# Swapping the partition halves that the second head group's projection reads, in a fused Nyström attention and two-layer FFN kernel

## The chip, the cores and the metric

One core of a Trainium2 chip (trn2). The metric is the device time of one execution in microseconds (us). The engines are called as in the profile: PE is TensorE's matmuls, PEld its weight loads, DVE is VectorE, ACT is ScalarE, POOL is GpSimd, SP is SyncE, which here issues nearly all DMAs.

## The reference

q, k and v have the shape (4 batches, 8 heads, 576 rows, 64). Everything is float32.

```
q_lm, k_lm = means of q, k over runs of 18 rows        (32 landmarks)
A, Bm, C = softmax(q k_lm'), softmax(q_lm k_lm'), softmax(q_lm k')
Z = six Newton steps towards the inverse of Bm
x = A @ Z @ C @ v            -> 2304 tokens x 512
h = x @ moe_w_in  (512 x 2048);  g = h * tanh(softplus(h));  x = g @ moe_w_out
h = x @ moe2_w_in (512 x 2048);  g = h * sigmoid(h);         out = g @ moe2_w_out
```

## The kernel before, in words

The eight pairs of batch and head group (`Group`, line 1042; four heads in each, group 0 and group 1 of a batch) are worked through one after the other. For each, the kernel makes the 32 landmarks, the three softmaxes, the Newton steps, and at the end of `main` (lines 1284 to 1300) a small matrix per head, transposed: `ut_t[b][:, hg]` = (Z C v)' blocks of 64 rows by 32 columns. A head's block lies in one half of the 128 partitions: even heads in partitions 0 to 63, odd heads in 64 to 127. It is written by two matmuls into `pu`, one for the even heads and one for the odd, and one copy.

The attention output itself is never formed. Instead `projection` (lines 641 to 668) multiplies each head's 32 rows of Z C v with that head's 64 rows of `moe_w_in` (`w_t["a", ...]`, tile `wa`), for a block `fb` of 512 columns. The result, 4 heads x 32 = 128 partitions for each of the two groups `e`, goes to two PSUM banks `pp[0]` and `pp[1]` (tile `t` in the profile), is split there into a high and a low part (`wp`, by ACT or DVE), and is then the stationary operand against the softmax A (`at`) in `emit_h`. There are 4 batches x 4 blocks = 16 projections, each of 8 matmuls of 64 rows by 32 columns by 512: TensorE runs them on quarters of its columns and halves of its rows. Which row half a matmul uses follows from the partitions of its operands (`r`), and which column quarter from the partitions of its output (`32 * h`). In the order of the program, written as (row half, column quarter), a projection before runs (0,0) (1,1) (1,1) (0,2) (0,2) (1,3) (1,3) (0,0). Each float32 matmul is two instructions in the trace.

After attention starts, the first FFN layer (`emit_h`, `gated`, `emit_o`) fills TensorE between attention steps; partial sums go to DRAM (`yh`, `ys`). The second layer (`second_layer`, lines 896 to 915) runs one level of Strassen in a fixed order of matmuls.

The order of all other work is written out at build time by a planner (`Line`): it holds modelled times for each engine and for the DMA stream (`transfer`, line 259), and issues what is due. Engines then run their instructions in that order, and wait for data. `cost` (lines 103 to 108) gives a 64 x 32 matmul an eighth of the whole-array time. While attention runs and the model sees TensorE without work for a time, lines 1518 to 1526 insert pairs of transposes of `ident` into an unused bank (the instructions `y<-ident`, `h<-ident` and some `t<-ident` in the trace; nothing reads their output).

`loading` (lines 567 to 595) brings each weight from DRAM as 512 KB tiles of 128 partitions with one DMA each, from the SP queue. For `moe_w_in` there are 16 such tiles (`"a"`; `f = fb * 4 + kk`); kk = 0 and 1 hold group 0's heads, kk = 2 and 3 group 1's. The first two go to `wst`, the next four to `aw` (space that the softmax tiles use later), the rest to `wst`. `decode` (line 530) turns the loaded words into float32 in `wa` with ACT and DVE instructions.

The scores of the softmaxes A and C (`scores`, line 1122) also use 64 x 32 matmuls, 8 for each call, in the order (0,0) (1,1) (0,2) (1,3) (1,0) (0,1) (1,2) (0,3). The lines in the profile are those of the planner's helper: L256 is every computing instruction and L268 every DMA, so rows are told apart by tiles.

Of the kernel before, what the change touches and what calls it, by code (L numbers as in the profile page):

```python
# [55 lines left out]
def f32(ap):  # L56
    return ap.bitcast(FP32)


def width(ap):  # L60
    return ap.size() // ap.shape[0]


class Line:
# [194 lines left out]
    def transfer(self, engine, **kw):  # L259
        ap = kw["out"] if kw["out"].space == bass.MemoryType.SB else kw["in_"]  # L260
        start = max(self.now, self.free["D"], self.depend("D", "dma", kw))
        rate = 0.24e6 if ap.shape[0] < 128 else 0.4e6
        self.free["D"] = start + width(ap) * ap.shape[0] * 4 / rate
        end = self.free["D"] + 2.1
        self.end = max(self.end, end)
        self.last.add("D")
        self.record("D", kw, end)
        return engine.dma_start(**kw)  # L268
# [120 lines left out]
def kernel(  # L389
# [11 lines left out]
    nc = tc.nc  # L401
# [3 lines left out]
    LM = 32  # L405
# [3 lines left out]
    HG = 4  # L409
    GB = H // HG  # L410
# [3 lines left out]
    KD = DM // 128  # L414
# [12 lines left out]
    line = Ring.line = Line(nc)  # L427
# [11 lines left out]
    def slots(n, of, **kw):  # L439
# [30 lines left out]
        out=twice.rearrange("p (a d) -> p a d", a=2),  # L470
# [18 lines left out]
    def until(cond):  # L489
        while not cond():  # L490
            yield "W"

    def marked(*m):
        return lambda: all(a in marks for a in m)
# [4 lines left out]
    w_t, w_ready = {}, {}  # L499
# [10 lines left out]
    def place(o, l, f):  # L510

        if o == "a":
            fb = f // KD
            return wa_p, [] if fb < 2 else [("P", B - 1, fb - 2)]
        n = f if l == 0 else 2 * (f % HF) + f // HF
        if o == "i":
            i = 0 if n < HF else 1 + (n - HF) // (HF // 2)
            return wi_pools[i] if i < len(wi_pools) else None, []
        p = n // HF
        pool = w_pools[p][n % HF] if p in w_pools else None  # L520
        return pool, [] if l == 0 else [("last", n)]
# [45 lines left out]
    def loading():  # L567
        yield from until(marked(("load",)))
        for i, (o, l, f) in enumerate(w_order):
            yield from until(lambda: sum((w not in w_ready) for w in w_order[:i]) < LOADS)  # L570
            wst = None
            if o == "a":
                if f < 2 or not lent:
                    yield from until(wst_r.any)
                    wst = wst_r.take([128, 512, 2], I32)
                    a = wst[0]
                else:
                    a = lent.pop(0)
                fb, kk = divmod(f, KD)
                src = weights[l][0][kk * 128:(kk + 1) * 128, fb * 2 * FB:(fb + 1) * 2 * FB]  # L580
            elif o == "i":
                yield from until(lambda: place(o, l, f)[0] is not None and wst_r.any())
                wst = wst_r.take([128, 512, 2], I32)
                a = wst[0]
                src = weights[l][0][:, f * 256:(f + 1) * 256].rearrange("(k p) n -> p k n", p=128)
            else:
                yield from until(lambda: place(o, l, f)[0] is not None and marked(*place(o, l, f)[1])())
                a = place(o, l, f)[0].tile([128, 512, 2], I32, tag="w", name="wst")
                src = weights[l][1][f * 128:(f + 1) * 128, :]
            if o == "i":  # L590
                line.transfer(nc.sync, out=a.rearrange("p (k n) t -> p k (n t)", k=KD), in_=src)
            else:
                line.transfer(nc.sync, out=a.rearrange("p n t -> p (n t)"), in_=src)
            decodes.append((i, line.add(decode(o, l, f, a, wst), "D", "A", line.end)))
            yield "W"
# [16 lines left out]
    a_t, a_ready, ut_t, wp_t, wp_ready = {}, {}, {}, {}, {}  # L612
# [20 lines left out]
    def projections():  # L633

        for half in range(2):
            for b in range(B):
                yield from until(marked(*((b, "ut", e) for e in range(GB))))
                for fb in (2 * half, 2 * half + 1):
                    yield from projection(b, fb)

    def projection(b, fb):
        keys = [("a", 0, fb * KD + kk) for kk in range(KD)]
        yield from until(lambda: wp_r.any() and all(w_ready.get(k, LATE) <= line.now for k in keys))
        yield from until(lambda: t_r.claim(GB))
        pp = [t_r.take([128, FB], FP32) for e in range(GB)]
        for i in range(HG):
            for e in range(GB):
                h = (i + e) % HG
                r = slice(64 * (h % 2), 64 * (h % 2) + 64)
                T.matmul(  # L650
                    out=pp[e][0][32 * h:32 * h + 32],
                    lhsT=ut_t[b][r, e, h // 2, :],
                    rhs=f32(w_t[keys[2 * e + h // 2]])[r, :],
                    start=True,
                    stop=True,
                )
        marks.add(("P", b, fb))
        wp_ = wp_t[b, fb] = wp_r.take([128, 2, GB, FB], F32R)
        wp = wp_[0]
        yield "W"  # L660
        for e in range(GB):
            VA.copy(out=wp[:, 0, e], in_=pp[e][0])
        yield "V"
        for e in range(GB):
            V.tensor_tensor(out=wp[:, 1, e], in0=pp[e][0], in1=f32(wp[:, 0, e]), op=ALU.subtract)
            Ring.give(pp[e])
        wp_ready[b, fb] = line.end + 0.12 + SLACK
        yield "W"
# [373 lines left out]
    class Group:  # L1042
# [215 lines left out]
        def newton(self):  # L1258

            yu, g = self.yu, self.g  # L1260
            bd = self.bd.rearrange("p h l -> p (h l)")
            whole = g > 1
            for it in range(6):
                lo = 0 if it < 5 else LM
                if whole:
                    yield "V"
                    self.blocks(yu[:, 0:LM], 1.0)
                    yield "T"
                yield from until(self.banks.open)
                pn = self.banks.take([128, LM + D], FP32)  # L1270
                if whole:
                    T.matmul(out=pn[0][:, lo:], lhsT=bd, rhs=yu[:, lo:], start=True, stop=True)
                else:
                    self.each(pn[0][:, lo:], yu[:, 0:LM], yu[:, lo:])
                yield "V"
                yn = s_p.tile([128, LM + D], FP32, tag="yu", name="yu", bufs=4)
                V.scalar_tensor_tensor(
                    out=yn[:, lo:], in0=yu[:, lo:], scalar=2.0, in1=pn[0][:, lo:], op0=ALU.mult, op1=ALU.subtract
                )
                Ring.give(pn)  # L1280
                yu = yn
                yield "T"
            yield "V"
            self.blocks(self.bn, self.rc)
            yield "T"
            yield from until(self.banks.open)
            pu = self.banks.take([128, HG // 2 * LM], FP32)
            for e in range(2):
                T.matmul(
                    out=pu[0][64 * e:64 * e + 64].rearrange("p (i l) -> p i l", l=LM),  # L1290
                    lhsT=yu[:, LM:],
                    rhs=self.bd[:, e::2],
                    start=True,
                    stop=True,
                )
            yield "W"
            VA.copy(out=ut_t[self.b][:, self.hg].rearrange("p i l -> p (i l)"), in_=pu[0])
            Ring.give(pu)
            yield "W"
            marks.add((self.b, "ut", self.hg))  # L1300
            yield from until(marked((g, "a_t")))
            marks.add((g, "done"))
# [150 lines left out]

    line.add(attention(), "C")
    line.add(loading(), "S")
    line.add(projections(), "X")
    line.add(inputs(), "S")
# [8 lines left out]
    def o_time(u):  # L1466
        ph, t, f, first, last = u
        if first and not y_r.any_of(KD):
            return LATE
        return max(g_ready.get((ph, t, f), LATE), w_ready.get(("o", 0, f), LATE))  # L1470
# [4 lines left out]
    while todo or flight:  # L1475
# [15 lines left out]
        if f_r is not None and len(later) and wp_r.any():  # L1491
# [3 lines left out]
            n = 4 * TH if name else 2 * TH  # L1495
# [12 lines left out]
        to = o_time(flight[0]) if flight else LATE  # L1508
# [23 lines left out]
        ph, t, f, first, last = u  # L1532
# [56 lines left out]
```

## Time and profile before

| | |
|---|---|
| median of 3 runs | 850.13 us (850.02 to 850.81) |
| the profiled execution | 849.0 us |
| its span, first to last instruction | 847.2 us |
[...]
| PE busy | 828.9 us (98%), 5922 instructions |
| DVE, ACT, POOL busy | 532.3, 445.1, 281.8 us |
| DMA | 72.31 MB, mean 85 GB/s |

The page of the profile gives each engine's busy time, the span in slices, and the chain of waits: from the last instruction back to what released it, or to the instruction before it on its engine. In a chain or a timeline, "PE t L256 x16" is 16 instructions in a row that write tile `t`. A window's line gives each engine's busy time in a stretch. Matmul ends are modelled, so durations of overlapping small matmuls say less than the starts of what follows them.

### The profile page before, as it was taken

How to read it: one execution, taken by the hardware profiler on the slowest of the kernel's cores; microseconds unless marked ns; L12 is line 12 of the kernel's file. 1: busy time of each engine (PE TensorE's matmuls, PEld its weight loads, DVE VectorE, ACT ScalarE, POOL GpSimd, SP SyncE). 2: the span in 40 equal slices, each digit the busy share in tenths (PEclk: the TensorE clock that was granted, in tenths of full speed). 3: DMA queues.
4: the chain of work that ended last, by engine and by line, in shares of the span. 5: the costliest groups of instructions: out<-in, count | busy, mean ns of one | idle time of the engine just before them, and what ended most of it. 6: DMA issues, size and time to landing. Idle time of an engine off the chain costs nothing.

```text
span 847.2 us, 15580 instructions
## 1 busy us (share of the span) xinstructions
PE 828.9 (98%) x5922; PEld 735.2 (87%) x5922; DVE 532.3 (63%) x1088; ACT 445.1 (53%) x979; POOL 281.8 (33%) x324
## 2 busy tenths in 40 slices
PE   8999999999999999999999999999999999999997
PEld 6687978878899898989899898988888988998885
DVE  7968665664477787434407999877555567555542
ACT  6576765747465655433435665554444444544422
POOL 3323533442345565415333244221223221232210
PEclk9999999999999999999999999999999999999999
DMA  9664114200145465331117223101300000200002
GB/s 297 233 208 132 59 55 141 79 8 30 47 160 185 146 212 176 111 113 52 52 57 226 97 83 107 38 1 50 102 0 1 1 1 11 65 1 1 1 2 74
DMA packets 41483, 72.31 MB, mean 85 GB/s; under 512 B 4288, under 2 KB 30912, under 8 KB 41408
## 3 DMA queue, kind: packets, MB, share of 16 engines
q1 hardware_dynamic: 40832, 70.53, 26.1%
q8 instruction: 46, 0.75, 0.4%
q10 hardware_dynamic: 576, 0.79, 0.3%
q14 instruction: 29, 0.24, 0.1%
HBM read 57.15 MB, written 14.16 MB: 84 GB/s over the span
## 4 chain that ended last, share of the span: by engine, by line
PE 91%; DVE 3%; DMA 2%; ACT 2%; issue 1%; SPq 1%; DVEq 0%; ACTq 0%
PE y L256 49%; PE h L256 32%; PE t L256 10%; DMA wp<-in_q_dram 1%; SPq L268 1%; DVE z L256 0%; ACT z L256 0%; DMA wst<-ys 0%; DMA out_dram<-ysb 0%; DVE wa L256 0%; DVE at L256 0%; DVE nm L256 0%; ACT wp L256 0%; DVE asm L256 0%; ACT ysb L256 0%
## 5 line engine op out<-in xcount | busy, mean ns | idle before, releaser
L256 PE MATMUL y<-g,wo 128*128 128x288 f32 x1536 | 229.6, 300 | 0.0
L256 PEld LDWEIGHTS y<-g,wo 128*128 128x128 f32 x1536 | 209.0, 189 | 12.4 <-issue 11.3
L256 PE MATMUL y<-wo,xg 128*128 128x512 f32 x693 | 179.8, 395 | 0.0
L256 POOL TENSOR_TENSOR g<-z,g 128x288 fp32r<-128x288 f32 x127 | 112.7, 901 | 155.6 <-ACT g L256 114.5
L256 PEld LDWEIGHTS y<-wo,xg 128*128 128x128 f32 x693 | 128.6, 188 | 20.8
L256 DVE TENSOR_TENSOR z<-h,z 128x384 f32<-128x384 f32 x162 | 88.5, 554 | 67.6 <-PE h L256 65.0
L256 PE MATMUL h<-at,wp 128*128 128x288 f32 x768 | 120.8, 302 | 3.9 <-ACT z L256 3.7
L256 PEld LDWEIGHTS h<-at,wp 128*128 128x128 f32 x768 | 106.3, 188 | 12.1 <-ACT z L256 6.2
L256 ACT ACTIVATE z<-h 128x288 f32<-128x288 f32 x128 | 51.8, 413 | 70.4 <-PE h L256 65.6
L256 ACT ACTIVATE z<-z 128x384 f32<-128x384 f32 x94 | 49.4, 525 | 39.8 <-DVE z L256 39.4
L256 POOL TENSOR_TENSOR wo<-m,wo 128x512 fp32r<-128x512 f32 x32 | 47.3, 1480 | 47.6 <-ACT wo L256 39.6
L256 PE MATMUL h<-xg,wp 128*128 128x384 f32 x288 | 58.0, 336 | 1.5 <-DVE z L256 1.5
L256 PE MATMUL h<-xg,wf 128*128 128x384 f32 x288 | 57.7, 336 | 0.2 <-DVE z L256 0.2
L256 DVE TENSOR_TENSOR xg<-z,xg 128x384 fp32r<-128x384 f32 x75 | 43.2, 576 | 21.0 <-ACT xg L256 20.9
L256 DVE SCALAR_TENSOR_TENSOR m<-wst,m 128x512 int32<-128x512 int32 x64 | 55.4, 873 | 0.7
L256 PEld LDWEIGHTS h<-xg,wp 128*128 128x128 f32 x288 | 51.2, 188 | 5.1 <-DVE z L256 1.9
L256 PEld LDWEIGHTS h<-xg,wf 128*128 128x128 f32 x288 | 51.3, 188 | 3.6 <-DVE z L256 0.5
L256 ACT CAST g<-z 128x288 fp32r<-128x288 f32 x116 | 48.6, 435 | 8.7 <-PE y L256 7.5
L256 POOL TENSOR_TENSOR wf<-m,wf 128x256 fp32r<-128x256 f32 x20 | 15.2, 762 | 91.3 <-ACT wf L256 86.6
L256 PE MATMUL y<-wo,wp 128*128 128x512 f32 x171 | 44.9, 395 | 0.0
L256 DVE TENSOR_TENSOR wp<-t,wp 128x512 fp32r<-128x512 f32 x32 | 20.6, 685 | 33.6 <-ACT wp L256 33.6
L256 ACT ACT_TABLE_LOAD x31 | 39.8, 1283 | 3.3 <-PE h L256 2.0
(234 smaller groups left out, 1228.5 us busy)
## 6 DMA issues: line engine op xcount, KB each, us to landing
wst<-in_moe_w_out_dram SPq DMA_DIRECT2D x32, 512.0 KB, 6.0
wst<-in_moe_w_in_dram SPq DMA_DIRECT2D x28, 512.0 KB, 4.5
kn<-in_k_dram SPq DMA_DIRECT2D x8, 576.0 KB, 7.1
vn<-in_v_dram SPq DMA_DIRECT2D x8, 576.0 KB, 6.4
yh<-ysb SPq DMA_DIRECT2D x32, 144.0 KB, 1.8
ysb<-yh SPq DMA_DIRECT2D x32, 144.0 KB, 2.9
ys<-ysb SPq DMA_DIRECT2D x32, 144.0 KB, 2.2
qn<-in_q_dram SPq DMA_DIRECT2D x7, 576.0 KB, 4.8
```

Of the source, the lines that this page charges most:

```text
L256: r = getattr(self.nc[e], name)(**kw)
L268: return engine.dma_start(**kw)
```

## The change

The second group's weight rows (kk >= 2) are loaded with their two partition halves swapped, by two DMAs of 64 partitions instead of one of 128; the second group's `ut` blocks are written to the opposite halves by its two `pu` matmuls; and the projection takes, for group e and head i, the half (i + e) % 2. The projection's matmuls are then (0,0) (1,0) (1,1) (0,1) (0,2) (1,2) (1,3) (0,3). The planner's DMA model gives its lower rate only to transfers of exactly 96 partitions, no longer to all below 128; the other such transfers are the new halves (64) and the stores of the result (`send`, 32).

```diff
     def transfer(self, engine, **kw):
...
-        rate = 0.24e6 if ap.shape[0] < 128 else 0.4e6
+        rate = 0.24e6 if ap.shape[0] == 96 else 0.4e6
...
             if o == "i":
                 line.transfer(nc.sync, out=a.rearrange("p (k n) t -> p k (n t)", k=KD), in_=src)
+            elif o == "a" and kk >= KD // GB:
+                for e in range(2):
+                    to = a[64 * e:64 * e + 64].rearrange("p n t -> p (n t)")
+                    line.transfer(nc.sync, out=to, in_=src[64 - 64 * e:128 - 64 * e])
             else:
...
         for i in range(HG):
             for e in range(GB):
-                h = (i + e) % HG
-                r = slice(64 * (h % 2), 64 * (h % 2) + 64)
+                r = slice(64 * ((i + e) % 2), 64 * ((i + e) % 2) + 64)
                 T.matmul(
-                    out=pp[e][0][32 * h:32 * h + 32],
-                    lhsT=ut_t[b][r, e, h // 2, :],
-                    rhs=f32(w_t[keys[2 * e + h // 2]])[r, :],
+                    out=pp[e][0][32 * i:32 * i + 32],
+                    lhsT=ut_t[b][r, e, i // 2, :],
+                    rhs=f32(w_t[keys[2 * e + i // 2]])[r, :],
...
             for e in range(2):
+                r = slice(64 * ((e + self.hg) % 2), 64 * ((e + self.hg) % 2) + 64)
                 T.matmul(
-                    out=pu[0][64 * e:64 * e + 64].rearrange("p (i l) -> p i l", l=LM),
+                    out=pu[0][r].rearrange("p (i l) -> p i l", l=LM),
```

## Rows read from the trace of the kernel before

**Rows 1.** The page: busy us of each engine, share of the span, instructions.

```profile
PE 828.9 (98%) x5922; PEld 735.2 (87%) x5922; DVE 532.3 (63%) x1088; ACT 445.1 (53%) x979; POOL 281.8 (33%) x324
```

**Rows 2.** Windows: stretch, length, busy PE, PEld, DVE, ACT, POOL, clock, DMA share, GB/s.

```profile
40.00:130.00 90.00, 88.73 (x908) 75.20 (x898) 62.86 (x164) 63.47 (x125) 36.13 (x39) 1.00 0.36 113
130.00:230.00 100.00, 97.91 (x960) 82.90 (x960) 56.36 (x169) 60.99 (x134) 35.52 (x42) 1.00 0.17 51
230.00:410.00 180.00, 178.29 (x1338) 163.23 (x1337) 106.12 (x147) 88.56 (x206) 84.91 (x82) 1.00 0.45 146
470.00:600.00 130.00, 129.78 (x647) 116.38 (x646) 109.57 (x208) 72.34 (x156) 36.77 (x39) 1.00 0.23 71
```

**Rows 3.** The chain of waits over the whole span, by line.

```profile
by line: PE y L256 48.6%; PE h L256 32.2%; PE t L256 10.2%; issue 1.2%; DMA wp<-in_q_dram 0.9%; SPq L268 0.5%; DVE z L256 0.5%; ACT z L256 0.5%; DMA wst<-ys 0.4%; DMA out_dram<-ysb 0.4%; DVE wa L256 0.4%; DVE at L256 0.4%; DVE nm L256 0.3%;
```

**Rows 4.** The tile wa: all projection matmuls, ns min/median/max, first and last start.

```profile
L256 PE MATMUL t<-wa,ut x256: 588/590/614, 39.4 to 407.7; 64*32 64x512 f32 x128
```

**Rows 5.** The chain in order of time (start, us, what): six of the 16 projections.

```profile
39.49 1.86 PE t L256 x16
...
73.38 2.03 PE t L256 x16
...
123.98 1.86 PE t L256 x16
...
130.13 1.86 PE t L256 x16
...
177.68 1.96 PE t L256 x16
...
406.45 1.96 PE t L256 x16
```

**Rows 6.** Timeline of the weight loads around the projection at 222.6 us (start, us).

```profile
222.64 0.17 PEld L256 LDWEIGHTS t<-wa,ut 64*32 64x32 f32 x8 [0.16 <-issue]
223.10 0.14 PEld L256 LDWEIGHTS t<-wa,ut 64*32 64x32 f32 x4 [0.29 <-issue]
223.53 0.14 PEld L256 LDWEIGHTS t<-wa,ut 64*32 64x32 f32 x4 [0.29 <-issue]
224.51 0.97 PEld L256 LDWEIGHTS y<-g,wo 128*128 128x128 f32 x7 [0.84 <-issue]
```

**Rows 7.** Timeline of the weight loads of A's scores at 206.5 us.

```profile
206.49 0.18 PEld L256 LDWEIGHTS t<-Tq,lmT 64*32 64x32 f32 x16 [0.16 <-issue]
```

**Rows 8.** The chain at two calls of the scores, C's and then A's.

```profile
195.49 0.90 PE t L256 x16
...
206.56 0.65 PE t L256 x16
```

**Rows 9.** The tile ident: the inserted transposes, ns min/median/max, first and last start.

```profile
L256 PE MATMUL y<-ident x144: 271/273/474, 1.4 to 134.4; 128*128 128x128 f32 x144
L256 PE MATMUL h<-ident x86: 271/273/422, 1.8 to 128.2; 128*128 128x128 f32 x86
```

**Rows 10.** The chain behind the first projection, and behind the one at 177.7 us.

```profile
41.35 2.99 PE y L256 x26
...
179.64 0.68 ACT wp L256 x2
```

**Rows 11.** Timeline of SP in the first 90 us: loads of aw and what follows.

```profile
5.01 0.45 SPq L268 DMA_DIRECT2D aw<-in_moe_w_in_dram  x1
...
21.50 1.72 SPq L268 DMA_DIRECT2D aw<-in_moe_w_in_dram  x1
23.27 2.17 SPq L268 DMA_DIRECT2D wst<-in_moe_w_out_dram  x4
```

**Rows 12.** The chain at 29.6 us: a decode of wa.

```profile
29.60 0.67 DVE wa L256
```

**Rows 13.** The chain in the second layer: the wait for the next tokens.

```profile
598.87 3.74 DMA wst<-ys
```

**Rows 14.** The window around that wait.

```profile
600.00:610.00 10.00, 8.51 (x42) 7.21 (x41) 5.62 (x11) 3.33 (x8) 2.94 (x4) 1.00 0.32 90
```

## Prediction

> **What bounds the kernel now.** I read the page first: PE is busy for 828.9 of 847.2 us, and no other engine for more than 63% [rows 1]. That alone could be inserted or overlapping work, so the second view is the windows by stage: from 130 to 230 us PE is busy 97.91 of 100, from 230 to 410 it is 178.29 of 180 with DVE, ACT and POOL near or under 60%, and from 470 to 600 it is 129.78 of 130, with DVE at 109.57 behind it [rows 2]. The third is the chain of waits: PE lines are 91% of it, the tile `t` alone 10.2% [rows 3]. So what shortens PE's own work shortens the end, unless something just behind PE takes over.
>
> The changed matmuls are the 256 instructions that read `wa` and `ut` [rows 4], 16 to a projection. Each of the 16 projections is one piece of the chain, 1.86 us where nothing else is merged into it [rows 5]. Their listed 590 ns each is a modelled end of overlapping work; I take the time from the starts of the loads instead. At 222.64 eight weights are loaded, at 223.10 four more, at 223.53 four more, and the next layer's load starts at 224.51 [rows 6]. So four instructions run at a time, a wave lasts 223.53 - 223.10 = 0.43 us for 512 columns, and 1.86 = 4 x 0.43 + 0.14.
>
> **The change, part by part.**
>
> *The projection's order.* By the list of (row half, column quarter), the eight matmuls before use four places of the array, each twice; a float32 matmul is two instructions, so each place has four to run: four waves. After, the eight use eight places, each two instructions: two waves, if eight places run at once. The scores do that already: all 16 weights of A's scores are loaded within 0.18 us [rows 7], and the 16 instructions take 0.65 us of the chain [rows 8]. At 288 columns a wave should take 0.43 x 288 / 512 = 0.24; two are 0.48, and 0.17 is left for getting in and out. A projection then takes 2 x 0.43 + 0.14 to 0.17 = 1.00 to 1.03 us and saves 0.83 to 0.86; I take 0.85. The bound below: C's scores, which read with a stride, take 0.90 [rows 8], so a wave is (0.90 - 0.17) / 2 = 0.365, 1.51 times as long. If eight contiguous streams slowed that much, a projection would take 2 x 0.65 + 0.17 = 1.47 and save 0.39. I take 0.85, since the projection reads without a stride as A's scores read in runs of 32. More than 0.86 is excluded while a wave is 0.43.
>
> *How much of it reaches the end.* Twelve projections start from 177.68 on, the last at 406.45 [rows 5]. There the inserted transposes are over (last at 134.4) [rows 9], PE is at 98 to 99% [rows 2], and the others follow PE: behind the projection at 177.68 the chain goes to ACT's split of its result [rows 10], which starts when the projection ends and so moves with it. I count them in full: 12 x 0.85 = 10.2. Four start before (39.49, 73.38, 123.98, 130.13) [rows 5], where transposes were inserted because the planner saw PE idle. The planner already prices the projection at eight at once, so there PE gets closer to its plan and may begin to wait for attention's steps. Kept: between 0 and 0.85 each. I take 0.6: behind the first projection 26 inserted transposes still run for 2.99 us [rows 10], and the chain stays on PE, so what comes next was not the bound; but its slack is unknown. 4 x 0.6 = 2.4. Sum 12.6.
>
> *The loads.* Eight of the 16 `moe_w_in` tiles become two DMAs. SP takes 0.45 us for one such issue, and 1.72 at worst [rows 11]: 8 x 0.45 = 3.6 us more of SP. Behind the one at 21.50 on SP stand the four `moe_w_out` loads [rows 11]. They and the other tiles are used long after; the one place where the chain passes a decode of these tiles is at 29.60 [rows 12], where ACT and DVE run in order, so a late half would hold Newton's steps. No row shows a load of 64 partitions. Bounds 0 (the bytes are the same) and 1.72; I take 0.3, most of one issue, because the chain touches it once. The planner's price is unchanged (two halves at 0.4e6 are one whole), so the order of work before the first stores should stay.
>
> *The planner's rate.* The result's stores of 32 partitions (64 KB) are modelled at 0.16 us instead of 0.27. PE's order in the second layer is fixed by its loops; DVE, ACT and POOL may get another order after the first stores, near 590 us. There the chain waits 3.74 us for tokens that SP issued among those stores [rows 13], and PE loses 10 - 8.51 = 1.49 us [rows 14]. I take 0, bounds -1.5 (that gap goes) and +1.5 (as much again). The `pu` matmuls only swap places: two instructions as before, 0.
>
> **Sum.** Against the profiled execution's 849.0: 849.0 - 12.6 + 0.3 = 836.7. The median of the runs is 1.1 above that execution; 837.8.
>
> [...] In the trace, four matmuls run at once in every wave of a projection [rows 6]. By each place's own order, the first wave of before has quarters 1, 2 and 3 writing `pp[1]`, from both row halves; had the halves taken turns at that bank, more than four waves would be seen. [...]
>
> **Rivals.**
> 1. *No gain on PE*: the two halves take turns at each bank, four waves of 0.43 stay, the loads add 0.3: 850.4. For it: the scores never mix halves in a bank, so they do not exclude it. Against: the wave count above. 0.05.
> 2. *Swallowed*: the first six projections keep nothing because attention's chain ends last there, and DVE, at 84% from 470 to 600 [rows 2], gives up more: half of 10 x 0.85 and the 0.3 leave 850.1 - 4.0 = 846.1. Against: PE's 178.29 of 180 from 230 on. 0.05.
> 3. *Slower, by the order*: the new order puts two matmuls of one column quarter next to each other, which no row shows. If such neighbours cannot overlap and a waiting matmul holds those behind it, the groups are (0,0) | (1,0) (1,1) | (0,1) (0,2) | (1,2) (1,3) | (0,3): five, ten waves with both instructions, 10 x 0.43 + 0.14 = 4.44, and 16 x 2.58 = 41 us more: 892. It decides from the fifth wave on. Against it: before, neighbours share a whole place; a strict hold would make four groups, eight waves and 3.6 us, and 1.86 is measured. 0.04. [...] Slower through the loads alone, 852 and more, would need the PE gain to fail too: 0.02.
>
> **How the numbers follow.** The forecast has 0.84, with 0.02 of it below the range. Low end: 16 x 0.86 = 13.8, no cost of loads, the gap of 1.5 gone: 850.1 - 15.3 = 834.8. High end: only twelve projections, each saving 0.62 (midway between 0.39 and 0.85), 7.4, less 1.7 for the loads: 850.1 - 5.7 = 844.4. A measurement here can tell 0.2%, 1.7 us, from no change. Faster by more: 0.84 + 0.05 = 0.89; same 0.05; slower 0.06.
>
> **What would show it.** Right: a projection's chain piece of about 1.0 us; all its 16 weights loaded in one stretch near 0.2 us, then the next load about 1.0 us after the first; the second half of the span about 12 us earlier; PE's sum of busy time down by about that. Wrong: loads still in steps 0.43 apart (rival 1); new waits of PE on ACT or DVE between 40 and 230 us, or more idle PE from 470 on (rival 2); projections over 1.9 us (rival 3); a later decode near 29.6 us (loads).

## The result, and the profile after

The median of the changed kernel is 836.4 us (four executions, 835.59 to 837.28) against 850.08 us of the kernel before on the same chip (four, 848.75 to 850.81): a ratio of 0.9841, 95% interval 0.9823 to 0.9859. The forecast was 837.8 us. The profiled execution took 837.18 us, its span is 835.4 us: 11.8 us less than before.

The first line of the page, beside [rows 1]: the number of PE's instructions is the same, their busy time is 12.9 us less.

```profile
PE 816.0 (98%) x5922; PEld 730.0 (87%) x5922; DVE 531.6 (64%) x1087; ACT 445.9 (53%) x980; POOL 282.1 (34%) x324
```

The timeline of the weight loads around one projection, beside [rows 6]: all 16 weights go in within 0.18 us, and the next layer's load starts 218.68 - 217.66 = 1.02 us after the first. Before it was 224.51 - 222.64 = 1.87. So eight places run at once, in two waves of the 0.43 us of before (2 x 0.43 + 0.16), and a projection saves 0.85 us.

```profile
217.66 0.18 PEld L256 LDWEIGHTS t<-wa,ut 64*32 64x32 f32 x16 [0.17 <-issue]
218.68 0.69 PEld L256 LDWEIGHTS y<-g,wo 128*128 128x128 f32 x5 [0.84 <-issue]
```

A trap is in the view by tile. One matmul of the projection is listed at 601 ns here and at 590 before [rows 4]: by that alone the change made them slower. The ends are modelled; the starts of the loads behind them tell the time.

```profile
L256 PE MATMUL t<-wa,ut x256: 589/601/613, 39.0 to 397.3; 64*32 64x512 f32 x128
```

Where it was kept. PE's instructions stand in the same order in both traces, so the starts of the same projection can be subtracted, both read from PE's timeline. There the projections of before start 0.07 us ahead of their pieces of the chain in [rows 5]; these are four of them, the 1st, 8th, 9th and 16th.

```profile
39.42 1.93 PE L256 MATMUL t<-wa,ut 64*32 64x512 f32 x16
...
231.60 1.93 PE L256 MATMUL t<-wa,ut 64*32 64x512 f32 x16
...
244.77 1.93 PE L256 MATMUL t<-wa,ut 64*32 64x512 f32 x16
...
406.38 1.93 PE L256 MATMUL t<-wa,ut 64*32 64x512 f32 x16
```

And these are the six projections of [rows 5] after, with the 8th and the 9th.

```profile
38.96 1.09 PE L256 MATMUL t<-wa,ut 64*32 64x512 f32 x16
...
72.49 1.25 PE L256 MATMUL t<-wa,ut 64*32 64x512 f32 x16
...
122.25 1.09 PE L256 MATMUL t<-wa,ut 64*32 64x512 f32 x16
...
127.56 1.09 PE L256 MATMUL t<-wa,ut 64*32 64x512 f32 x16
...
174.31 1.09 PE L256 MATMUL t<-wa,ut 64*32 64x512 f32 x16
...
225.75 1.09 PE L256 MATMUL t<-wa,ut 64*32 64x512 f32 x16
...
240.47 1.09 PE L256 MATMUL t<-wa,ut 64*32 64x512 f32 x16
...
396.81 1.09 PE L256 MATMUL t<-wa,ut 64*32 64x512 f32 x16
```

| projection | start before - start after | gained since the row above |
|---|---|---|
| 1st | 39.42 - 38.96 = 0.46 | 0.46 (ahead of any projection) |
| 2nd | 73.31 - 72.49 = 0.82 | 0.36 by one projection |
| 3rd | 123.91 - 122.25 = 1.66 | 0.84 by one |
| 4th | 130.06 - 127.56 = 2.50 | 0.84 by one |
| 5th | 177.61 - 174.31 = 3.30 | 0.80 by one |
| 8th | 231.60 - 225.75 = 5.85 | 2.55 by three |
| 9th | 244.77 - 240.47 = 4.30 | -1.55 by one |
| 16th | 406.38 - 396.81 = 9.57 | 5.27 by seven |

Eleven times 0.84 is 9.2, so about 3.0 us got lost between the 5th and the 16th projection, 2.4 of them between the 8th and the 9th. The windows agree, beside [rows 2] and [rows 14]: from 230 to 410 us PE is busy 175.62 of 180, 2.67 less than before. From 470 to 600 it is now busy all the time, and from 590 to 600, the stretch that holds before's gap of 1.49 us, there is no gap.

```profile
130.00:230.00 100.00, 97.89 (x985) 85.11 (x984) 58.12 (x172) 62.75 (x139) 35.84 (x43) 1.00 0.20 63
230.00:410.00 180.00, 175.62 (x1358) 165.57 (x1357) 107.91 (x150) 92.56 (x215) 90.16 (x88) 1.00 0.43 137
470.00:600.00 130.00, 130.00 (x648) 116.48 (x647) 107.46 (x201) 72.25 (x155) 35.54 (x40) 1.00 0.24 74
590.00:600.00 10.00, 10.00 (x51) 8.85 (x50) 7.35 (x14) 4.44 (x11) 3.64 (x5) 1.00 0.20 56
```

So the span's 11.8 us are made of 9.57, one more projection (0.84) and the gap that is gone (1.5): 11.9, with 0.1 lost elsewhere. Two places want an explanation.

The first is the timeline of all engines from 229 to 236 us. Read it upwards: PE waits 0.88 and 1.00 us, the latter for POOL's product `g`; POOL had waited 3.92 us for ACT's `g`; and ACT had waited 3.28 us at a decode of `wa` for the DMA of a `moe_w_in` tile. That `g` stands behind the decode in ACT's order: its input `z` was written by 229.25 + 0.41 = 229.66 us, and it starts at 233.51. The tile is one of the eight that now come in two halves.

```profile
229.25 0.41 ACT L256 ACTIVATE z<-h 128x288 f32<-128x288 f32 x1
...
232.95 0.66 ACT L256 ACTIVATE wa<-wst 128x512 f32<-128x512 f32 x1 [3.28 <-DMA wst<-in_moe_w_in_dram]
233.51 0.42 ACT L256 CAST g<-z 128x288 fp32r<-128x288 f32 x1
...
233.98 0.40 PE L256 MATMUL y<-g,wo 128*128 128x288 f32 x1 [0.88 <-ACT g L256]
...
234.06 2.49 POOL L256 TENSOR_TENSOR g<-z,g 128x288 fp32r<-128x288 f32 x2 [3.92 <-ACT g L256]
...
235.38 0.80 PE L256 MATMUL y<-g,wo 128*128 128x288 f32 x4 [1.00 <-POOL g L256]
```

The second is the second layer's wait for tokens [rows 13]. Before, SP issues that load at 598.87 us, behind a run of twelve stores of the result; now at 586.33, behind a run of only eight, with the twelve after it. Counted from the load of tokens ahead of it on SP (592.41 before, 582.02 now) it comes 4.31 us later instead of 6.46. DVE's subtraction on the tokens starts at 590.20, and PE goes on without a gap. SP before:

```profile
593.28 5.49 SPq L268 DMA_DIRECT2D out_dram<-ysb  x12
598.87 0.39 SPq L268 DMA_DIRECT2D wst<-ys  x1
```

And after, with DVE:

```profile
582.55 3.69 SPq L268 DMA_DIRECT2D out_dram<-ysb  x8
586.33 0.38 SPq L268 DMA_DIRECT2D wst<-ys  x1
586.82 5.55 SPq L268 DMA_DIRECT2D out_dram<-ysb  x12
...
590.20 0.96 DVE L256 TENSOR_TENSOR wst<-wst 128x768 f32<-128x768 f32 x1 [1.32 <-DMA wst<-ys]
```

Theory: the order of the projection's matmuls is worth about 12 us; the planner's rate moved the tokens' load and gives 1.5 us and more; the halves of the loads take some of it back through ACT. Rivals: the gap near 600 closed because PE arrived earlier, not by the rate; the stall at 233 us comes from PE's earliness, not from the halves; and the order itself, not the set of places in use, made the two waves.

### The profile page after: what moved, and what is told of

Same layout as the page of the kernel before. It is cut to its first block, busy times and chain, and to the rows that moved or that the text cites. A ratio compares the mean times of both kernels' runs of the same rounds, so it can differ in the third digit from the quotient of the medians.

```text
span 835.4 us, 15597 instructions
## 1 busy us (share of the span) xinstructions
PE 816.0 (98%) x5922; PEld 730.0 (87%) x5922; DVE 531.6 (64%) x1087; ACT 445.9 (53%) x980; POOL 282.1 (34%) x324
## 4 chain that ended last, share of the span: by engine, by line
PE 58%; DVE 1%; ACT 1%; DMA 0%; issue 0%; DVEq 0%; ACTq 0%
PE y L256 33%; PE h L256 24%; DVE z L256 0%; DMA out_dram<-ysb 0%; PE t L256 0%; ACT z L256 0%; ACT wp L256 0%; DVE wf L256 0%; ACT wf L256 0%; ACT ysb L256 0%; DVE wp L256 0%; ACT g L256 0%; DVE ysb L256 0%; DVE xg L256 0%; DVE m L256 0%
## 5 line engine op out<-in xcount | busy, mean ns | idle before, releaser
L256 DVE TENSOR_TENSOR ysb<-y,ysb 128x288 f32<-128x288 f32 x32 | 13.2, 457 | 42.6 <-PE y L256 42.6
```

The costliest lines, as they stand in the source:

```text
L256: r = getattr(self.nc[e], name)(**kw)
```

## The experiments

**The order alone.** Only the diff's part in `projection`; the rows and `ut` stay where they are, so group 1's heads are mixed up in pairs.

```diff
-                h = (i + e) % HG
-                r = slice(64 * (h % 2), 64 * (h % 2) + 64)
+                r = slice(64 * ((i + e) % 2), 64 * ((i + e) % 2) + 64)
...
-                    out=pp[e][0][32 * h:32 * h + 32],
+                    out=pp[e][0][32 * i:32 * i + 32],
```

> The projection's new order alone; group 1's weights and ut stay in their old halves, so in that group each head's place gets its neighbour's product (the output is not the reference's). Theory: the order is worth 16 x 0.84 = 13.4 us less 0.4 behind the first projection, so 850.1 - 13.0 = 837.1; with whole loads PE does not stall at about 234 us, and the stall near 600 us is back, since the old rate stays. Rival A, that the stall at 234 us comes from PE being early and not from the half loads: the stall is there, and about 839. Rival B, that the stall near 600 us went because of PE's earlier time and not by the rate: it is gone here too, about 835.4.

Measured: 836.6 us against 849.13, ratio 0.9856 [0.9842, 0.9869]: 12.2 us less. (Differences from here on are the ratio times the time before; the medians differ by 12.5.) The timelines of this kernel show the 16 loads in one stretch, and that ACT's wait near 231 us is 1.64 us and POOL's `g` costs PE 0.50. Its window from 590 to 600 us has the gap of 1.49 us.

```profile
217.84 0.18 PEld L256 LDWEIGHTS t<-wa,ut 64*32 64x32 f32 x16 [0.16 <-issue]
...
231.48 0.67 ACT L256 ACTIVATE wa<-wst 128x512 f32<-128x512 f32 x1 [1.64 <-DMA wst<-in_moe_w_in_dram]
```

```profile
590.00:600.00 10.00, 8.51 (x41) 7.17 (x41) 6.85 (x13) 4.08 (x9) 2.60 (x4) 1.00 0.10 31
```

The order makes nearly all of the gain. The gap near 600 stays with PE early, so earliness didn't close it. Of PE's 1.88 us of waiting at 233 us earliness alone makes 0.50 here, and 0 to 0.8 in the profiles of the later kernels with whole loads; the rest comes with the halves.

**The halves alone.** Before, with the second group's tiles in two DMAs, not swapped; the rate stays as it was for the stores.

```diff
-        rate = 0.24e6 if ap.shape[0] < 128 else 0.4e6
+        rate = 0.24e6 if ap.shape[0] in (96, 32) else 0.4e6
...
+            elif o == "a" and kk >= KD // GB:
+                for e in range(2):
+                    to = a[64 * e:64 * e + 64].rearrange("p n t -> p (n t)")
+                    line.transfer(nc.sync, out=to, in_=src[64 * e:64 * e + 64])
```

> Only the second group's loads in two DMAs of 64 partitions each, not swapped; all else as before, the order of the planner's work too. Theory: PE is later at 234 us than after the change, so the later landing is covered: 850.1 to 850.6, with the fourth tile's landing about 1 us later after its first issue than before (6.3 us). Rival A, half loads cost nothing anywhere: 850.1 and the landing at 6.3 us. Another, that transfers of 64 partitions run at half speed: 852 or more.

Measured: 850.3 us, ratio 1.0016 [1.0007, 1.0025]: 1.4 us more (0.6 to 2.1). The timeline shows it near 31 us, the place that the prediction named: ACT waits 2.12 us for a tile, Newton's next step comes late, and PE waits 1.76 us, where before it waits 0.48. The profiled execution is one of the slower ones (851.96; the eleven lie between 849.36 and 852.77), so not every execution need stall as long.

```profile
31.44 0.67 ACT L256 ACTIVATE wa<-aw 128x512 f32<-128x512 f32 x1 [2.12 <-DMA aw<-in_moe_w_in_dram]
...
33.68 0.37 PE L256 MATMUL t<-yu 32*32 32x96 f32 x8 [1.76 <-DVE yu L256]
```

**The rate alone, and all but the rate.** The first is before with the new rate; the second is the changed kernel with the old rate for stores.

```diff
-        rate = 0.24e6 if ap.shape[0] < 128 else 0.4e6
+        rate = 0.24e6 if ap.shape[0] == 96 else 0.4e6
```

> Only the planner's rate for transfers below 128 partitions other than 96. Theory: DVE's operation on the next tokens is put behind work that PE waits for, PE's 1.5 us stall near 600 us goes, 848.5. Rival B, the rate does nothing: 850.1 and the stall stays.

```diff
-        rate = 0.24e6 if ap.shape[0] == 96 else 0.4e6
+        rate = 0.24e6 if ap.shape[0] in (96, 32) else 0.4e6
```

> The whole change, but stores of 32 partitions keep the old modelled rate. Theory: 836.4 + 1.6 = 838.0, with the stall near 600 us back. Rival B: 836.4 and no stall there.

Measured: the rate alone 847.04 us, ratio 0.9978 [0.9969, 0.9986], 1.9 us less; all but the rate 837.9 us, ratio 0.987 [0.9854, 0.9885], which is 1.2 us above the order alone, though the intervals overlap. The windows settle it. With the rate alone, the stretch of [rows 14] has no gap:

```profile
600.00:610.00 10.00, 10.00 (x51) 8.86 (x50) 7.35 (x14) 4.47 (x11) 3.65 (x5) 1.00 0.22 62
```

Without the rate, the changed kernel has the 1.49 us back, ten microseconds earlier:

```profile
590.00:600.00 10.00, 8.51 (x42) 7.26 (x41) 6.01 (x12) 3.61 (x9) 2.94 (x4) 1.00 0.27 89
```

So the rate closes the gap, whenever PE arrives.

**The same places without new loads.** If what matters is that eight places are in use, the swap of partitions isn't needed: group 1's results can go to other column quarters. Here a head keeps its row half, its output in `pp[1]` moves on by one quarter, and group 1's scores of A are turned by one quarter, so that both operands of the next matmul agree. With the new rate; the loads and `ut` are those of before.

```diff
-        for i in range(HG):
+        for h in range(HG):
...
-                h = (i + e) % HG
+                to = (h + e) % HG
...
-                    out=pp[e][0][32 * h:32 * h + 32],
+                    out=pp[e][0][32 * to:32 * to + 32],
...
+                    to = (h + (0 if i else self.hg)) % HG
...
-                        out=s[e][0][32 * h:32 * h + 32, 0:SH],
+                        out=s[e][0][32 * to:32 * to + 32, 0:SH],
```

> A version without half loads: the loads and ut stay as before; group 1's products go to the next column quarter (head i in quarter i + 1), and the scores of softmax A of group 1 are written to the same turned quarters, so that the rows still meet. Eight places for eight matmuls again, and the planner's new rate. Theory (order and rate give, the half loads take): 0.9856 and 0.9978 together, 0.983 of before, about 835.0, 0.5 to 1.5 below the change itself; a projection takes 1.02 us, PE's stall at 234 us is near 0.6 us instead of 1.9. Rival (half loads cost nothing once PE is early): as the change, 0.984.

Two more kernels vary the order of the program. In the first the eight matmuls of the turned kernel come half by half: four of rows 0 to 63, then four of rows 64 to 127.

```diff
-        for h in range(HG):
-            for e in range(GB):
+        for half in range(2):
+            for n in range(HG):
+                e, h = n % 2, 2 * (n // 2) + half
```

> As the version with turned scores, but the projection's eight matmuls in another order of the program: the four of row half 0 first, then the four of row half 1, so neighbours share a row half and never a quarter. Theory (each place has its own order and nothing holds the others): two waves, 1.02 us, and the same time. Rival (weights load beside running matmuls only in another row half, or a matmul that waits holds all behind it): a projection of 1.4 us or more, and at least 6 us more.

In the second, which is before otherwise, the two matmuls of each place follow one another: four places, each used twice.

```diff
-        for i in range(HG):
+        for h in range(HG):
...
-                h = (i + e) % HG
```

> The kernel before, with the two matmuls of each place directly behind one another in the program: (0,0) (0,0) (1,1) (1,1) (0,2) (0,2) (1,3) (1,3). Theory (each place has its own order): still four waves, 1.86 us for a projection, 849 to 850. Rival (strict order of the program): the second of each pair holds the others, more than four waves, at least 2.7 us a projection and 13 us more.

Measured: turned 834.3 us against 848.78, ratio 0.983 [0.9817, 0.9844]; half by half, one execution, 834.95 us; pairs in a row, one execution, 849.23 us. The weight loads, half by half: one stretch, 219.22 - 218.20 = 1.02 us.

```profile
218.20 0.18 PEld L256 LDWEIGHTS t<-wa,ut 64*32 64x32 f32 x16 [0.16 <-issue]
219.22 0.43 PEld L256 LDWEIGHTS y<-g,wo 128*128 128x128 f32 x3 [0.84 <-issue]
```

And pairs in a row: eight, four and four as in [rows 6], 224.99 - 223.12 = 1.87 us.

```profile
223.12 0.17 PEld L256 LDWEIGHTS t<-wa,ut 64*32 64x32 f32 x8 [0.16 <-issue]
223.58 0.15 PEld L256 LDWEIGHTS t<-wa,ut 64*32 64x32 f32 x4 [0.28 <-issue]
224.01 0.15 PEld L256 LDWEIGHTS t<-wa,ut 64*32 64x32 f32 x4 [0.28 <-issue]
224.99 1.08 PEld L256 LDWEIGHTS y<-g,wo 128*128 128x128 f32 x8 [0.84 <-issue]
```

Neither order moves the number of waves, two in 1.02 us and four in 1.87: in these kernels it is the number of matmuls on the busiest place, times two instructions. In all of them each row half has four matmuls and each column quarter two, so here it is the pair of both that counts. Were a waiting matmul to hold back those behind it, pairs in a row would make five groups by the prediction's way of counting, ten waves, 10 x 0.43 + 0.14 = 4.44 us a projection; 1.87 is measured.

**What the halves cost beside the order.** The changed kernel again and the turned one again, on one chip; with them, the turned kernel with all 16 tiles in two halves, not swapped (the lines of "the halves alone" without `and kk >= KD // GB`).

```diff
+            elif o == "a":
+                for e in range(2):
+                    to = a[64 * e:64 * e + 64].rearrange("p n t -> p (n t)")
+                    line.transfer(nc.sync, out=to, in_=src[64 * e:64 * e + 64])
```

> The changed kernel itself, beside the version with turned scores on one chip. Theory: 0.984 of before, 835.6 where before is 849.1, and about 1 us above the turned version; PE stalls at about 234 us for 1.5 to 2.3 us, and in some profiles near 32 us as well. Rival: within 0.3 us of the turned version.

> The version with turned scores and whole loads, for the comparison on one chip. Theory: 0.983 of before, 834.5. Rival (half loads cost nothing): as the change.

> The version with turned scores, but all 16 tiles of the first projection weights loaded in two halves of 64 partitions (not swapped): 16 more DMAs than the turned version, 8 more than the change. Theory (each half load delays a landing that an engine's queue waits for in order): 1 to 3 us above the turned version, at least as slow as the change. Rival (half loads cost nothing): as the turned version.

Measured against 849.14 us: turned 834.86, ratio 0.9831 [0.9818, 0.9844]; the change 837.42, ratio 0.986 [0.9848, 0.9873]; all in halves 840.89, ratio 0.9902 [0.9883, 0.9922]. With 0, 8 and 16 tiles in halves the time is 0, 2.5 and 6.0 us over the turned kernel. The last is more than the 1 to 3 us expected, and the least certain: its six executions run from 838.11 to 844.42 us, at mean granted clocks from 0.998 down to 0.992, and the profiled one is the fastest. The turned version beats both kernels.

How much a kernel pays differs between executions. With whole loads the first projection starts at 38.65 to 39.84 us in every profile; with halves it starts at 38.96 and 41.60 in the two profiles of the change, and at 40.21 to 41.18 in the other three so far. So the stall near 31 us comes and goes: the change's second profile has it (ACT waits 2.02 us there, PE 1.56), its first does not. At the place near 233 us PE, once early, waits 0 to 0.8 us with whole loads and 1.0 to 1.9 with halves.

Why a half is dear is in the windows of the backlog, where the DMA engines have no idle time (the last two columns are their busy share and GB/s). Before, with whole tiles:

```profile
53.00:55.20 2.20, 2.20 (x28) 1.41 (x27) 1.14 (x3) 2.17 (x6) 1.15 (x2) 1.00 1.06 417
```

The changed kernel, with four halves:

```profile
52.00:56.80 4.80, 4.80 (x47) 4.01 (x46) 3.53 (x14) 4.74 (x10) 1.40 (x3) 1.00 1.03 256
```

All in halves:

```profile
54.00:56.00 2.00, 2.00 (x26) 1.21 (x25) 1.18 (x4) 1.97 (x6) 0.86 (x2) 1.00 1.05 234
```

The same holds ahead of the stall near 233 us. From 228 to 232 us, first the order alone, then the change:

```profile
228.00:232.00 4.00, 4.00 (x33) 4.00 (x32) 2.76 (x4) 2.31 (x6) 0.81 (x1) 1.00 0.99 378
```

```profile
228.00:232.00 4.00, 4.00 (x32) 4.00 (x31) 2.58 (x4) 1.60 (x4) 0.82 (x1) 1.00 1.01 256
```

The engines are just as busy and move 0.56 to 0.68 as much. In the first backlog, before, the two tiles of 512 KB issued at 45.61 and 46.13 us landed 8.4 and 9.1 us later, 1.2 us apart; after, the four halves of 256 KB issued at 44.52, 45.04, 45.73 and 46.32 landed 8.5, 9.1, 9.7 and 10.5 us later, 1.1 to 1.4 us apart. Here a half took as long as a whole tile.

**The old rate for halves.** If a half moves at 256 GB/s, the planner's old 0.24 MB per us was right for it, and told so it might place the decodes later.

```diff
-        rate = 0.24e6 if ap.shape[0] == 96 else 0.4e6
+        rate = 0.24e6 if ap.shape[0] in (96, 64) else 0.4e6
```

> The change, but the planner models the half loads of 64 partitions at the lower rate again (0.24 instead of 0.4 MB per us; the stores of 32 keep the new rate), so that it writes the decodes of these tiles later into ACT's and DVE's order. The whole plan is written anew by it. Theory (the half loads cost because the plan puts a decode ahead of its landing, in engines that run in order): most of the 2.5 us against the turned version comes back, 0.983 to 0.985, and ACT's waits for these tiles fall from 6 to 8 us to near 3. Rival (the halves cost by the transfers themselves): 0.986 as the change.

Measured: 839.96 us, ratio 0.99 [0.9884, 0.9917], slower than the change, so the theory missed. ACT's wait for these tiles did fall, from 5.9 to 2.9 us in all, but the plan got another shape: 126 inserted transposes into `h` instead of 86 [rows 9].

```profile
L256 PE MATMUL h<-ident 128*128 128x128 f32 x126 | 20.2, 294 | 0.1
```

The truer price of one transfer did not help by itself here; whether a plan with that price and the order of the change would regain the 2.5 us stays open.

**Which partitions, or how many DMAs.** All in halves again, but the two DMAs of a tile take its even and its odd partitions. The number of rows, the bytes and the number of DMAs are the same; which rows of DRAM one DMA reads changes with the partitions.

```diff
-                    to = a[64 * e:64 * e + 64].rearrange("p n t -> p (n t)")
-                    line.transfer(nc.sync, out=to, in_=src[64 * e:64 * e + 64])
+                    to = a[e::2].rearrange("p n t -> p (n t)")
+                    line.transfer(nc.sync, out=to, in_=src[e::2])
```

> The version with the scores turned and all 16 tiles of moe_w_in in two DMAs of 64 partitions (840.9 us, ratio 0.9902 [0.9883, 0.9922], 227 GB/s in its backlog at full DMA share), with one thing changed: the two DMAs of a tile take its even and its odd partitions, not its lower and upper half. Rows per DMA, bytes, row length, number of issues and the planner's price are the same. Theory A (64 neighbouring partitions of one half are what makes a half tile as slow as a whole one): the loads move at near 417 GB/s in the backlog, and the time goes back to that of the turned version, 834.3 to 835.5, ratio near 0.983. Theory B (it is the number of DMAs or their 64 rows): the backlog stays near 230 to 260 GB/s and the time stays at 839 to 842, ratio 0.988 to 0.992. Between the two, near 837.5, both have a part.

Measured: 841.73 us, ratio 0.9909 [0.9893, 0.9926], so by the time theory B. The transfers say A: the same four loads, issued 0.6 us apart from 51.55 us on, land 7.7 to 7.8 us after their issues, hence 0.6 us apart, and the window around their landings moves 418 GB/s.

```profile
59.00:61.00 2.00, 2.00 (x28) 1.52 (x27) 0.73 (x3) 1.99 (x5) 0.98 (x2) 1.00 1.05 418
```

The time is spoilt by a wait that neither theory had. ACT's first decode of an `aw` tile starts at 23.84 us without a wait where all tiles are in lower and upper halves; here it waits 5.06 us, to 27.71, although that tile's own two DMAs (issued from 7.43 us on) had landed by 19.2 us. It starts when the next pair, issued from 21.11 us on, has landed. Newton's step behind it keeps PE idle for 4.74 us, and PE's granted clock, 1.00 from 20 to 25 us, is 0.84 from 25 to 30 and 0.50 from 30 to 35.

```profile
27.71 0.66 ACT L256 ACTIVATE wa<-aw 128x512 f32<-128x512 f32 x1 [5.06 <-DMA aw<-in_moe_w_in_dram]
...
28.80 0.54 PE L256 MATMUL t<-yu 32*32 32x96 f32 x8 [4.74 <-ACT yu L256]
```

```profile
30.00:35.00 5.00, 5.00 (x37) 4.40 (x36) 4.03 (x9) 1.99 (x5) 1.21 (x1) 0.50 1.03 408
```

So the low rate, 234 to 256 GB/s against 418, goes here with which 64 partitions one DMA fills (and which rows of DRAM it reads), and its whole price in time was not measured this way. A part of it shows: the first projection starts at 45.99 us, 5.48 later than with all in lower and upper halves, but near the second place ACT waits 1.50 us and PE 0.37, no more than with whole tiles (ACT 1.16 to 1.90, PE 0 to 0.8). Why the decode waits for the later pair is open: both tiles are parts of one larger tile (`words`, line 629 of that kernel), and no run tells whether the build ties them together where a DMA takes every second partition.

## Why the prediction was right

*The projection's order:* right, 1.02 us for a predicted 1.00 to 1.03, two waves for four. *How much reaches the end:* 12.2 us measured for 12.6. The first four kept 0.36, 0.84, 0.84 and 0.80, 2.84 in all for an assumed 2.4. Of the later ones, assumed in full, the order alone keeps 8.62 us by eleven (177.61 - 174.52 = 3.09 at the fifth, 406.38 - 394.67 = 11.71 at the sixteenth), 0.7 short of 11 x 0.85: it loses that where PE catches up with ACT near 233 us.

*The loads:* the step that failed. "The bytes are the same" gave 0.3 and a bound of 1.72; measured are 1.4 us alone and 1.2 to 2.5 beside the order. The price lies in the transfer more than in SP's 0.45 us for an issue: 256 GB/s instead of 417, each half landing 1.1 to 1.4 us after the one ahead of it, where a whole tile took 1.2, and ACT's next work behind it (3.28 us of waiting). The place near 29.6 us was named rightly; the one near 233 us was not seen, since before PE has no wait there to show.

The runs give the rate of a DMA into 64 neighbouring partitions as 234 to 256 GB/s, 0.56 to 0.61 of the whole tile's 417, and into every second one as 418. The prediction had no row of such a load.

*The planner's rate:* 0 was taken, with -1.5 as a bound; measured is -1.9 (-1.2 to -2.6). The lower bound, "that gap goes", was what happened: the rate sets where the planner puts the tokens' load among the stores, and at the new one it stands behind a run of eight of them instead of twelve. The prediction had that row and should have asked which way a cheaper store moves the load.

*The sum:* -12.2 + 1.4 - 1.9 = -12.7 from the parts, -13.5 and -11.9 from the two measurements of the whole. The errors at loads and rate, +0.9 to +2.2 and -1.9, nearly cancel. The order's term was right by its mechanism; that 837.8 came so close was luck in the other two.

*Rivals:* no gain on PE is out, since both halves write each bank and 16 weights go in at once. Slower by order is out by both kernels with another order, one execution each. Swallowed is out by the table; DVE, at 107.46 of 130 us from 470 to 600, has not become the bound. In the change's order two matmuls of one column quarter also stand next to each other; its projection takes 1.02 us, two waves.

## What to carry to other kernels

For small matmuls that share TensorE, count the instructions on the busiest pair of row half and column quarter: that number times the time of a wave (0.43 us), and 0.15 to 0.16 us, was the cost here, in each order of the program that was run (1.02 us for two, 1.87 for four). Places can be freed by turning an output by a column quarter as well as by moving an input to other partitions; the first costs no transfer (834.86 us against 837.42, on one chip). Before one DMA is split by partitions, measure what rate the pieces get (here 234 to 256 GB/s against 417), and see which engine's next work stands behind their landing (here ACT's, 3.28 us).

## What was not expected

A DMA of 256 KB into 64 neighbouring partitions took as long as one of 512 KB into 128 (1.1 to 1.4 us against 1.2, in a backlog), while its engines showed as fully busy: the share of busy DMA said nothing of the rate here (1.03 at 256 GB/s, 1.06 at 417). A change of a modelled rate, of no weight in the hardware, moved one load ahead of four stores and was worth 1.9 us. Where a stall falls differs between executions of one kernel, so a single profile of the change hid the stall near 31 us that its second profile shows.
